# Linear attention and channel mix on one core: queries and attention outputs turned by the transposing DMA

## The chip, the cores and the metric

One core of a Trainium2 chip runs the whole program. The metric is the device time of one execution in microseconds (us); the median of three runs of the kernel before is 203.64 us.

The engines of the core, as the profile names them: PE multiplies matrices (its weight loads are PEld), DVE and ACT work element by element on rows of 128 partitions, POOL and SP here only issue DMAs (and POOL a few constants). PE writes to PSUM, a memory of eight banks, and DVE or ACT must carry its results to SBUF, the working memory. Each engine takes its instructions in order. Engines wait for each other through semaphores.

## The reference

Inputs: q, k, v of shape (8 batches, 8 heads, 576 tokens, 64), a norm vector g of 64, two mixing vectors and three weight matrices.

```python
kv  = einsum('bhsd,bhse->bhde', k, v)
out = einsum('bhsd,bhde->bhse', q, kv)
rms = sqrt(mean(out * out, axis=-1) + 1e-06)
x   = (out / rms * g_norm)            # then heads side by side: (8, 576, 512)

x_prev = x shifted by one token
xk = mu_k * x + (1 - mu_k) * x_prev
xr = mu_r * x + (1 - mu_r) * x_prev
k  = maximum(xk @ w_k, 0)             # 512 -> 1024
v  = (k * k) @ w_v                    # 1024 -> 512
r  = 1 / (1 + exp(-(xr @ w_r)))       # 512 -> 512
result = r * v                        # float32, (8, 576, 512)
```

## The kernel before

The eight batches, numbered 0 to 7 in the code, go one after the other through a pipeline, in bf16. A batch's 576 tokens are laid out as 64 places of 9 tokens: partition p holds tokens 9p to 9p+8, so a load has long rows. Two heads lie above each other in the partitions (64 rows each, "e"), four such pairs side by side. The short names are those of the order string:

- `ld`: load of k, v or q (0, 1, 2) of a batch, issued by POOL (L192), which casts float32 to bf16. Each of in_k, in_v, in_q has one buffer, so a load waits until the batch before it has been read.
- `kv`: k transposed times v on PE (L284), summed over the 9 token groups; `kvo` carries it to SBUF.
- `qt`: q turned on PE, 36 transposes of 64x64 per half (L298); `qto` carries the four quarters to the tile qT (L214 on ACT, L216 on DVE).
- `u`: qT times kv on PE (L320) in three parts; `sq` squares them on ACT (L325), `red` sums the squares on DVE (L329), `nw` are the steps of the inverse root on DVE (L338 to L351), `mul` multiplies u with the root and gives y (L361, DVE).
- `x0`, `x`: y turned on PE (L376), so that channels lie in the partitions; `xo`, `x0o` carry it to the tile xT with the factor g (L366 on ACT, L368 on DVE).
- `wrap` (L532) copies the token before each row's first; `dif` forms the difference of neighbours (L536), `sc` scales it by mu (L542 on ACT, L544 on DVE), `add` adds x (L559), which gives xk and xr.
- `K`: xk times w_k (L572), relu to rt (L564 on ACT, L566 on DVE); `ks` squares rt to sqk (L578, L580). `R`: xr times w_r (L594) and the sigmoid (L597). `V`: sqk times w_v (L604). `fin` multiplies the two (L617, DVE) and stores the result in two DMAs on SP (L620).

A string, ORDER, lists all steps in eight periods. It is written out by hand or by a planner, and nothing reorders it: each engine takes its share of the steps in this order, a step marked ' has its evacuation on DVE and not on ACT, and the digits behind = name the PSUM banks. DMAs are issued where their step stands: loads on POOL, stores on SP. A DMA queue of SP also waits, for every new DMA, until the eighth before it has landed, as eight semaphores go round. xT has two buffers, used by even and odd batches; y, kv and qT have two each, out_sb seven.

Batches 0 and 1 are treated in parts of their own (`qtc`, `uh`, `xh` and the like); the change reaches them only in the shape of a tile.

Of the kernel before, what the change touches and what calls it, by code (L numbers as in the profile page):

```python
# [9 lines left out]
FP32 = mybir.dt.float32  # L10
# [37 lines left out]
    mul.2.2.0 x0.2=70 x0o.2.0 kvo.3.0 V.1.5.0=4 ksp.1.1.4.6 V.1.7.0=2 xo.2.0.4.1' wrap.2 V.1.4.0=7 xo.2.0.4.0'  # L48
    V.1.4.1 x0o.2.1' V.1.5.1 dif.2 sc.2.0.0' sc.2.0.3 sc.2.1.3 qt.3.0=16 qto.3.0.1 sc.2.1.1 qto.3.0.0 fin.1.4
    sc.2.0.1' add.2.0.0 qt.3.1=50 qto.3.1.1 sc.2.0.2' add.2.0.1 sc.2.1.0' qto.3.1.0' kvo.3.1 V.1.6.0=7 V.1.6.1  # L50
    """,
# [5 lines left out]
    nw.3.7.8 ks.2.0' K.2.7.0=1 mul.3.2.0 V.1.8.1 mul.3.1.1 K.2.7.1=4 ks.2.7 x0.3=62 mul.3.0.0 x0o.3.1 ks.2.1'  # L57
    mul.3.1.0 kv.4=51 mul.3.0.1 x.3.0.4=30 xo.3.0.4.1 fin.1.8 x0o.3.0' kvo.4.1' ks.2.2' ld.2.4 qt.4.0=47
    qto.4.0.1' ks.2.5 qto.4.0.0 xo.3.0.4.0' wrap.3 dif.3 sc.3.0.0' qt.4.1=61 V.2.1.0=2 R.2.2=7 sc.3.0.3'
    kvo.4.0' qto.4.1.1' sc.3.0.2 qto.4.1.0 sc.3.1.2' sc.3.0.1' V.2.0.0=0 V.2.2.0=3 ld.0.5 ld.1.5 V.2.0.1  # L60
    add.3.0.0 V.2.1.1 sc.3.1.1 fin.2.0 u.4.1=47 u.4.0=51 sq.4.1.0 add.3.0.1 u.4.2=6 sq.4.2.0 sq.4.0.0 V.2.2.1
    fin.2.1 fin.2.2 sq.4.0.1 red.4.5.9
    """,
# [6 lines left out]
    u.5.1=75 ks.3.0' add.3.1.1 ks.3.5 fin.2.3 ks.3.7 xo.4.0.4.1' wrap.4 u.5.0=10 sq.5.1.1 sq.5.0.0 sq.5.0.1  # L70
    xo.4.0.4.0' dif.4 red.5.5.9 u.5.2=6 sq.5.2.0 R.3.4=2 R.3.5=4 V.3.4.0=3 V.3.4.1 sc.4.0.2 sc.4.1.0 sq.5.1.0
    sc.4.0.1' R.3.6=2 sc.4.0.0' fin.3.4 red.5.0.5 V.3.5.0=4 V.3.5.1 nw.5.0.1 nw.5.1.2 fin.3.5 nw.5.2.3 sc.4.1.2
    nw.5.3.4 nw.5.4.5 nw.5.5.6 add.4.0.0 nw.5.6.7 nw.5.7.8 mul.5.2.0 mul.5.1.0 R.3.7=3 sc.4.0.3 add.4.0.1
    sc.4.1.3 add.4.1.1 V.3.6.0=2 V.3.6.1 R.3.8=4 fin.3.6 mul.5.0.1 V.3.7.0=3 V.3.7.1
# [46 lines left out]
def kernel(  # L121
# [150 lines left out]
    def span(Ms):  # L272
        return slice(2 * Ms[0], 2 * Ms[-1] + 2)

    def kv(a):

        mine(a, "kv", [128, NHP, HD], BF16)
        kb, vb = x_in["k", a], x_in["v", a]
        ps = [take(("kv", a, e), [128, 2, HD], FP32, "ps_kv") for e in range(2)]
        for M in range(2):  # L280
            for j in range(G):
                for e in range(2):
                    for i in range(2):
                        nc.tensor.matmul(ps[e][half(i), M, :], kb[half(e), 2 * M + i, tok(j)],  # L284
                                         vb[half(e), 2 * M + i, tok(j)], start=(j == 0), stop=(j == G - 1))

    def kv_out(a, e, eng):
        evac(eng, at[a]["kv"].rearrange("p (M e) c -> p e M c", e=2)[:, e], give(("kv", a, e)))

    def qt(a, M):  # L290

        mine(a, "qT", [128, NHP, S], BF16)
        qb = x_in["q", a]
        ps = [take(("qt", a, M, e), [128, G, P], BF16, "ps_qt") for e in range(2)]
        for j in range(G):
            for e in range(2):
                for i in range(2):
                    nc.tensor.transpose(ps[e][half(i), j, :], qb[half(e), 2 * M + i, tok(j)], ident[half(e), half(e)])  # L298

    def qt_out(a, M, e, eng):  # L300
        evac(eng, at[a]["qT"][:, 2 * M + e, :], give(("qt", a, M, e)).rearrange("p j c -> p (j c)"))

# [7 lines left out]
    def u(a, part):  # L310

        t0, n = TILES[part]
        ps = [take(("u", a, part, i), [128, max(n, 1), NHP, HD], FP32, "ps_u") for i in range(2 if n else 1)]
        qT_, kv_ = at[a]["qT"], at[a]["kv"]
        for k_ in range(max(n, 1)):
# [252 lines left out]
    def km_part(b, fcs, c0, c1, dst, eng):  # L568
        ps = take("km", [128, len(fcs), c1 - c0], FP32, "ps_km")
        for n, fc in enumerate(fcs):  # L570
            for cc in range(NHP):
                nc.tensor.matmul(ps[:, n, :], wk_sb[:, cc, 128 * fc:128 * fc + 128], at[b]["xk"][:, cc, c0:c1],  # L572
                                 start=(cc == 0), stop=(cc == NHP - 1))
        relu(give("km"), dst, eng)
# [81 lines left out]
    def part_square(b, j, f0, f1, eng):  # L656
# [8 lines left out]
        "qto": lambda eng, a, M, e: qt_out(a, M, e, eng),  # L665
        "u": lambda eng, a, part: u(a, part),
        "sq": lambda eng, a, part, i: square(a, part, i),
# [87 lines left out]
```

## Time and profile before

| What | us |
|---|---|
| Median of three runs (203.59, 203.64, 206.1) | 203.64 |
| Span of the profiled execution, first to last instruction | 201.8 |
| PE busy | 194.5 |
| DVE busy | 164.2 |
| ACT busy | 134.6 |
| L298, transposes of q, busy by the page's reckoning (504 of them) | 6.2 |
| L376, transposes of y (252) | 6.1 |
| L320, u (240) | 5.9 |

Busy times of PE are sums over overlapping instructions of a pipeline: one 64x64 transpose lasts some 190 ns, but 72 of them in a row take about 0.7 us. So the chain of waits, whose pieces stand end to end, is the better measure of what a group of small products costs PE. The row of a group gives the number of instructions, the busy time, the mean of one in ns, and how long the engine stood idle before it and for whom. SP and POOL rows with a q (SPq, POOLq) are issues of DMAs.

### The profile page before, as it was taken

How to read it: one execution, taken by the hardware profiler on the slowest of the kernel's cores; microseconds unless marked ns; L12 is line 12 of the kernel's file. 1: busy time of each engine (PE TensorE's matmuls, PEld its weight loads, DVE VectorE, ACT ScalarE, POOL GpSimd, SP SyncE). 2: the span in 40 equal slices, each digit the busy share in tenths (PEclk: the TensorE clock that was granted, in tenths of full speed). 3: DMA queues.
4: the chain of work that ended last, by engine and by line, in shares of the span. 5: the costliest groups of instructions: out<-in, count | busy, mean ns of one | idle time of the engine just before them, and what ended most of it. 6: DMA issues, size and time to landing. Idle time of an engine off the chain costs nothing.

```text
span 201.8 us, 6347 instructions
## 1 busy us (share of the span) xinstructions
PE 194.5 (96%) x2683; PEld 116.6 (58%) x2683; DVE 164.2 (81%) x360; ACT 134.6 (67%) x281; POOL 27.2 (13%) x44
## 2 busy tenths in 40 slices
PE   7989999999999999999999999999999999999990
PEld 2446754755646766577545765666764565656450
DVE  1499987989998998999999898998969899564341
ACT  3388975869959868798974799675795561416030
POOL 7854103021021004003000040000000000000000
PEclk9999999999999999999999999999999999999999
DMA  6999999999979906991993429901141013420674
GB/s 215 213 206 206 204 206 207 206 184 205 217 119 216 207 27 102 201 256 13 180 238 90 105 27 207 228 1 28 32 107 39 13 40 69 104 52 14 139 164 106
DMA packets 21425, 27.23 MB, mean 135 GB/s; under 512 B 1804, under 2 KB 16404, under 8 KB 21396
## 3 DMA queue, kind: packets, MB, share of 16 engines
q0 software_dynamic: 14912, 16.19, 49.4%
q1 hardware_dynamic: 6164, 10.23, 18.7%
q10 hardware_dynamic: 320, 0.39, 0.9%
q8 instruction: 21, 0.34, 0.7%
q14 instruction: 8, 0.07, 0.1%
HBM read 33.56 MB, written 9.44 MB: 213 GB/s over the span
## 4 chain that ended last, share of the span: by engine, by line
PE 87%; DMA 4%; DVE 2%; POOL 1%; issue 1%; ACT 1%; ACTq 1%; DVEq 0%; POOLq 0%
PE ps_v L604 30%; PE ps_km L572 28%; PE ps_r L594 15%; DMA rt<-in_v_dram 4%; PE ps_qt L298 3%; PE ps_x L376 2%; PE ps_u L320 2%; PE ps_km L644 2%; PE ps_kv L284 2%; PE ps_warm L258 1%; ACTq L620 1%; POOL q L184 1%; ACT sq L486 1%; DVE sqk L580 1%; POOL rt L184 1%
## 5 line engine op out<-in xcount | busy, mean ns | idle before, releaser
L604 PE MATMUL ps_v<-wv_sb,sqk 128*128 128x512 bf16 x280 | 67.1, 379 | 0.3
L572 PE MATMUL ps_km<-xk,wk_sb 128*128 128x288 bf16 (+3 forms) x480 | 64.6, 285 | 0.0
L572 PEld LDWEIGHTS <-wk_sb 128*128 128x128 bf16 x480 | 45.8, 98 | 17.4 <-DVE xk L559 0.3
L564 ACT ACTIVATE rt<-ps_km 128x288 bf16<-128x288 f32 (+3 forms) x93 | 38.5, 431 | 25.2 <-PE ps_km L572 22.1
L604 PEld LDWEIGHTS <-sqk 128*128 128x128 bf16 x280 | 26.4, 98 | 28.9 <-DVE sqk L580 0.4
L594 PE MATMUL ps_r<-wr_sb,xr 128*128 128x512 bf16 x144 | 34.7, 379 | 0.0
L597 ACT ACTIVATE sig<-ps_r 128x512 bf16<-128x512 f32 x36 | 21.1, 609 | 17.5 <-PE ps_r L594 14.8
L617 DVE TENSOR_TENSOR out_sb<-ps_v,sig 128x512 f32<-128x512 f32 (+1 forms) x37 | 24.4, 670 | 7.6 <-ACT sig L597 5.7
L594 PEld LDWEIGHTS <-xr 128*128 128x128 bf16 x144 | 13.8, 98 | 14.6
L578 ACT ACTIVATE sqk<-rt 128x576 bf16<-128x576 bf16 (+2 forms) x27 | 19.5, 730 | 0.2
L542 ACT ACTIVATE m<-dx,cols 128x576 bf16<-128x576 bf16 (+1 forms) x22 | 16.6, 777 | 4.2 <-DVE dx L536 4.2
L329 DVE TENSOR_REDUCE ss<-sq 128x16 f32<-128x1024 bf16 (+1 forms) x12 | 15.9, 1346 | 1.9 <-ACT sq L325 1.8
L361 DVE TENSOR_TENSOR y<-ps_u,rs 128x512 bf16<-128x512 f32 (+1 forms) x30 | 17.2, 629 | 0.2
L580 DVE TENSOR_TENSOR sqk<-rt 128x576 bf16<-128x576 bf16 (+3 forms) x30 | 14.4, 494 | 3.1 <-ACT rt L564 2.9
L566 DVE TENSOR_SCALAR rt<-ps_km 128x288 bf16<-128x288 f32 (+3 forms) x27 | 12.3, 466 | 5.3 <-PE ps_km L572 5.3
L325 ACT ACTIVATE sq<-ps_u 128x512 bf16<-128x512 f32 (+1 forms) x30 | 14.6, 572 | 1.2 <-PE ps_u L320 1.2
L192 POOL DMA_DIRECT2D in_k<-in_k_dram x6 | 4.5, 743 | 79.4 <-PE ps_kv L284 56.1
L544 DVE TENSOR_SCALAR m<-dx,cols 128x576 bf16<-128x576 bf16 (+3 forms) x44 | 14.6, 357 | 0.2
L366 ACT ACTIVATE xT<-ps_x,cols 128x128 bf16<-128x128 bf16 (+3 forms) x17 | 9.1, 563 | 5.0 <-PE ps_x L376 4.9
L536 DVE TENSOR_TENSOR dx<-xT 128x2304 bf16<-128x2304 bf16 (+5 forms) x13 | 11.6, 895 | 0.9 <-ACT xT L366 0.3
L559 DVE TENSOR_TENSOR xr<-m,xT 128x1152 bf16<-128x1152 bf16 x16 | 11.9, 751 | 0.2
L559 DVE TENSOR_TENSOR xk<-m,xT 128x1152 bf16<-128x1152 bf16 (+2 forms) x16 | 10.9, 699 | 0.3
(76 smaller groups left out, 171.5 us busy)
## 6 DMA issues: line engine op xcount, KB each, us to landing
out_dram<-out_sb SPq DMA_DIRECT2D x68, 128.0 KB, 3.4
in_k<-in_k_dram POOLq DMA_DIRECT2D x6, 576.0 KB, 6.6
in_v<-in_v_dram POOLq DMA_DIRECT2D x6, 576.0 KB, 8.9
in_q<-in_q_dram POOLq DMA_DIRECT2D x6, 576.0 KB, 11.0
wk_sb<-in_moe_w_k_dram POOLq DMA_DIRECT2D x2, 512.0 KB, 9.6
sqk<-in_k_dram SPq DMA_DIRECT2D x1, 576.0 KB, 3.8
q<-in_q_dram POOLq DMA_DIRECT2D x2, 288.0 KB, 6.8
sqk<-in_v_dram SPq DMA_DIRECT2D x1, 576.0 KB, 4.7
```

The costliest lines, as they stand in the source:

```text
L329: DVE.tensor_reduce(out=ss[:, g0:g1], in_=sq[:, g0:g1], op=ALU.add, axis=AX.X)
L361: DVE.tensor_mul(out=y[:, g], in0=give(("u", a, part, i)), in1=rs[:, g].unsqueeze(3).to_broadcast([128, max(n, 1), NHP, HD]))
L542: eng.activation(out=out_, in_=in_, func=AF.Copy, scale=mu)
L559: DVE.tensor_add(out=dst, in0=m[:, hs, c0:c1], in1=x[:, hs, c0:c1])
L564: eng.activation(out=dst, in_=ps, func=AF.Relu)
L572: nc.tensor.matmul(ps[:, n, :], wk_sb[:, cc, 128 * fc:128 * fc + 128], at[b]["xk"][:, cc, c0:c1], start=(cc == 0), stop=(cc == NHP - 1))
L578: eng.activation(out=sqk[:, fcs, o:o + n], in_=src, func=AF.Square)
L580: eng.tensor_mul(out=sqk[:, fcs, o:o + n], in0=src, in1=src)
L594: nc.tensor.matmul(ps, xr[:, cc, 128 * t:128 * t + 128], wr_sb[:, cc, :], start=(cc == 0), stop=(cc == NHP - 1))
L597: ACT.activation(out=sig[b, t], in_=give("r"), func=AF.Sigmoid)
L604: nc.tensor.matmul(ps, sqk[:, fc, 128 * t:128 * t + 128], wv_sb[:, fc, :], start=(fc == 0), stop=(fc == NFC - 1))
L617: DVE.tensor_mul(out=o, in0=give(key), in1=sig[b, t][:, c])
```

## The change

Four things are changed together.

1. q of batches 3 to 7 (QD = 3) is no longer turned on PE. A step `qd` issues two transposing DMAs on SP's queue per batch, from in_q (128 partitions x 1152 columns, taken as nine groups of 128 columns) to qT. The steps `qt` and `qto` of these batches go: 360 PE transposes and 20 evacuations.
2. The turned q lies differently: which half of the partitions a token group lies in depends on whether its number is even. So u of these batches (`u_turned`) works in 64x64 quadrants, 72 products instead of 40, and needs kv in both halves of the partitions. kv becomes twice as large, and `kvs` fills its second part: two copies of 64x256 on DVE per batch, which cross to the other half of the partitions.
3. y of batches 4 and 5 (YD) is turned by ten transposing DMAs on SP each (`yd`): two for the first group of tokens, eight for the others. The steps `x`, `x0`, `xo`, `x0o` of these batches go: 72 PE transposes and eight evacuations.
4. A DMA can't multiply by g. So from batch 4 on (WG = 4) xT is left without g, and g goes into copies of w_k and w_r (`wkg_sb`, `wrg_sb`): `wg`, four pieces of 128x1024 and four of 128x512 on DVE, before K.4. The evacuations of xT of batches 6 and 7 become plain copies.

The instructions by engine: PE 2,683 products before and 2,411 after. SP gets 30 transposing DMAs between its stores, in this order: the stores of fin.0.0 to fin.0.3, `qd.3`, five fins (1.4 to 1.8), `qd.4`, fin.2.0 to fin.2.2, `qd.5`, `yd.4`, fin.2.3 and fin.3.4 to fin.3.7, `yd.5`, `qd.6`, fin.3.8 and fin.4.0, `qd.7`, and the others. On POOL the loads of q of batches 4 to 7 wait for the transposing DMAs of the batch before instead of for PE. On DVE, wrap.4 and wrap.5 wait for the last transposing DMA of y. Of ORDER, the steps around are left in place but for these.

The new functions and the places that use them:

```diff
+    QD, YD, WG = 3, (4, 5), 4
+
+    def kv_swap(a, i, eng):
+        kv_ = at[a]["kv"]
+        evac(eng, kv_[half(1 - i), 1], kv_[half(i), 0])
+
+    def q_turn(a, M):
+        qT_ = mine(a, "qT", [128, 2 * G, 128], BF16)
+        nc.sync.dma_start_transpose(out=qT_[:, G * M:G * M + G], in_=x_in["q", a][:, 2 * M:2 * M + 2].rearrange("p m x -> p (m x)"))
+
+    def u_turned(a, part):
...
+                    for h in range(2 if n else 1):
+                        b = G * (2 * (ct // 2) + i) + (2 * (t0 + k_) + 1 + h if n else 0)
+                        r = b % 2
+                        out_ = ps[i][half(h), k_, ct, :] if n else ps[0][half(i), 0, ct, :]
+                        nc.tensor.matmul(out_, qT_[half(r), b // 2, half(ct % 2)], kv_[half(r), 0 if r == i else 1, ct, :],
+                                         start=True, stop=True)
+
+    def y_turn(a):
+        y, x = at[a]["y"], xT[a % 2]
+        for i in range(2):
+            nc.sync.dma_start_transpose(out=x[:, i::2, P:2 * P], in_=y[half(i), 0].rearrange("p n d -> p (n d)"))
+        for t in range(NHP):
+            for i in range(2):
+                c0 = 2 * P + 128 * t
+                nc.sync.dma_start_transpose(out=x[:, i::2, c0:c0 + 128], in_=y[:, 1 + 2 * t + i].rearrange("p n d -> p (n d)"))
+
+    def weights(which, cc, eng):
+        dst, src = ((wkg_sb, wk_sb), (wrg_sb, wr_sb))[which]
...
+            eng.tensor_scalar(out=dst[:, cc], in0=src[:, cc], scalar1=g_sb, scalar2=None, op0=ALU.mult)
...
-    def move(eng, dst, src):
-        if eng is ACT:
+    def move(eng, dst, src, a=0):
+        if a >= WG:
+            evac(eng, dst, src)
+        elif eng is ACT:
             eng.activation(out=dst, in_=src, func=AF.Copy, scale=g_sb)
...
-                nc.tensor.matmul(ps[:, n, :], wk_sb[:, cc, 128 * fc:128 * fc + 128], at[b]["xk"][:, cc, c0:c1],
+                nc.tensor.matmul(ps[:, n, :], (wkg_sb if b >= WG else wk_sb)[:, cc, 128 * fc:128 * fc + 128], at[b]["xk"][:, cc, c0:c1],
...
-            nc.tensor.matmul(ps, xr[:, cc, 128 * t:128 * t + 128], wr_sb[:, cc, :],
+            nc.tensor.matmul(ps, xr[:, cc, 128 * t:128 * t + 128], (wrg_sb if b >= WG else wr_sb)[:, cc, :],
```

And in ORDER, around the two turned batches (the same places before and after):

```diff
-    sc.3.1.3' x0.4=40 qt.5.1=75 x0o.4.0 sc.3.1.0' add.3.1.0 qt.5.0=62 qto.5.0.1' ks.3.6 K.3.7.0=3 ld.0.6
-    K.3.7.1=4 qto.5.1.1 V.2.3.0=2 V.2.3.1 kvo.5.0 ks.3.1' x0o.4.1 ks.3.3' qto.5.1.0' x.4.0.4=34 qto.5.0.0
+    sc.3.1.3' qd.5.0 qd.5.1 sc.3.1.0' add.3.1.0 ks.3.6 K.3.7.0=3 ld.0.6 K.3.7.1=4 V.2.3.0=2 V.2.3.1 kvo.5.0
+    kvs.5.0' kvs.5.1' ks.3.1' ks.3.3' yd.4 u.5.1=75 ks.3.0' add.3.1.1 ks.3.5 fin.2.3 wg.0.2' wg.0.3' ks.3.7
...
-    add.4.1.0 x0.5=16 x.5.0.4=24 x0o.5.1 x0o.5.0 qt.6.1=03 kv.6=75 ld.0.7 qt.6.0=61 xo.5.0.4.1' wrap.5
-    xo.5.0.4.0 dif.5 ks.4.0 qto.6.1.1 K.4.6.1=4 ks.4.6 kvo.6.1' R.4.0=2 R.4.1=3 qto.6.1.0' V.3.8.0=4 sc.5.0.3'
+    add.4.1.0 yd.5 qd.6.0 qd.6.1 kv.6=75 ld.0.7 wrap.5 dif.5 ks.4.0 K.4.6.1=4 ks.4.6 kvo.6.1' R.4.0=2 R.4.1=3
+    V.3.8.0=4 sc.5.0.3' ks.4.5' sc.5.0.0' K.4.7.0=5 sc.5.0.2' sc.5.0.1' kvo.6.0 kvs.6.0' kvs.6.1' add.5.0.1
```

More of the change, by code (lines that the diff above doesn't have):

```diff
@@ L57 @@
     nw.3.7.8 ks.2.0' K.2.7.0=1 mul.3.2.0 V.1.8.1 mul.3.1.1 K.2.7.1=4 ks.2.7 x0.3=62 mul.3.0.0 x0o.3.1 ks.2.1'
[L58 to L62, printed above, removed]
+    mul.3.1.0 kv.4=51 mul.3.0.1 x.3.0.4=30 xo.3.0.4.1 fin.1.8 x0o.3.0' kvo.4.1' ks.2.2' ld.2.4 qd.4.0 qd.4.1
+    ks.2.5 xo.3.0.4.0' wrap.3 dif.3 sc.3.0.0' V.2.1.0=2 R.2.2=7 sc.3.0.3' kvo.4.0' kvs.4.0' kvs.4.1' sc.3.0.2
+    sc.3.1.2' sc.3.0.1' V.2.0.0=0 V.2.2.0=3 ld.0.5 ld.1.5 V.2.0.1 add.3.0.0 V.2.1.1 sc.3.1.1 fin.2.0 wg.0.0'
+    u.4.1=47 u.4.0=51 sq.4.1.0 add.3.0.1 u.4.2=6 sq.4.2.0 sq.4.0.0 V.2.2.1 fin.2.1 fin.2.2 wg.0.1' sq.4.0.1
+    red.4.5.9
     """,
@@ L287, in kv_out, with by_pair @@
     def kv_out(a, e, eng):
[L288 removed]
+        evac(eng, at[a]["kv"][:, 0].rearrange("p (M e) c -> p e M c", e=2)[:, e], give(("kv", a, e)))
+    def kv_swap(a, i, eng):
[5 more added lines that the diff above has]
+    def u_turned(a, part):
+        t0, n = TILES[part]
+        ps = [take(("u", a, part, i), [128, max(n, 1), NHP, HD], FP32, "ps_u") for i in range(2 if n else 1)]
+        qT_, kv_ = at[a]["qT"], at[a]["kv"]
+        for k_ in range(max(n, 1)):
+            for ct in range(NHP):
+                for i in range(2):
[10 more added lines that the diff above has]
+        for t in range(NHP):
+            for i in range(2):
+                c0 = 2 * P + 128 * t
+                nc.sync.dma_start_transpose(out=x[:, i::2, c0:c0 + 128], in_=y[:, 1 + 2 * t + i].rearrange("p n d -> p (n d)"))
+    def weights(which, cc, eng):
+        dst, src = ((wkg_sb, wk_sb), (wrg_sb, wr_sb))[which]
+        if eng is ACT:
+            ACT.activation(out=dst[:, cc], in_=src[:, cc], func=AF.Copy, scale=g_sb)
+        else:
+            eng.tensor_scalar(out=dst[:, cc], in0=src[:, cc], scalar1=g_sb, scalar2=None, op0=ALU.mult)
+    def by_pair(qT_):
+        return qT_.rearrange("p c x -> p (c x)").rearrange("p (n s) -> p n s", n=NHP)
     def qt(a, M):
[L292 removed]
+        mine(a, "qT", [128, 2 * G, 128], BF16)
         qb = x_in["q", a]
@@ L665 @@
         "qto": lambda eng, a, M, e: qt_out(a, M, e, eng),
-        "u": lambda eng, a, part: u(a, part),
+        "u": lambda eng, a, part: (u_turned if a >= QD else u)(a, part),
+        "kvs": lambda eng, a, i: kv_swap(a, i, eng),
+        "qd": lambda eng, a, M: q_turn(a, M),
+        "yd": lambda eng, a: y_turn(a),
+        "wg": lambda eng, which, cc: weights(which, cc, eng),
         "sq": lambda eng, a, part, i: square(a, part, i),
```

61 lines of the change are left out of this document (31 added, 30 removed).

## The prediction

> **What bounds the kernel now.** The list of cores gives a span of 201.8 us at a granted TensorE clock of 0.998, so nothing is throttled. The page's first part and its chain come next:
>
> ```profile
> PE 194.5 (96%) x2683; PEld 116.6 (58%) x2683; DVE 164.2 (81%) x360; ACT 134.6 (67%) x281; POOL 27.2 (13%) x44
> ...
> PE 87%; DMA 4%; DVE 2%; POOL 1%; issue 1%; ACT 1%; ACTq 1%; DVEq 0%; POOLq 0%
> ```
>
> From 33 us to 193 us the chain lists PE pieces alone, end to end: what leaves PE shortens the kernel, if nothing else arrives late. The second thing to read is how near that is. The busy times by stretch:
>
> ```profile
> core 0: us, PE busy (x) PEld busy (x) DVE busy (x) ACT busy (x) POOL busy (x), PEclk, DMA share, GB/s
> ...
> 83.00:112.00 29.00, 29.00 (x413) 17.91 (x412) 27.61 (x57) 22.60 (x50) 2.23 (x3) 1.00 0.79 157
> ```
>
> DVE is busy 27.61 of 29.00 us in the stretch that prepares K.4: it is hardly less of a bound there than PE. The chain in that stretch (start, length, what) prices the removed work and shows its neighbours:
>
> ```profile
> 93.61 0.17 PE ps_x L376 x4
> 93.78 0.71 PE ps_qt L298 x72
> ...
> 97.30 0.57 PE ps_x L376 x32
> 97.87 0.71 PE ps_u L320 x40
> ...
> 109.91 6.37 PE ps_km L572 x52
> 116.28 0.63 PE ps_x L376 x36
> 116.91 0.41 PE ps_qt L298 x36
> ```
>
> **What goes (gain).** Batches are numbered from 0, as in the code. The chain's pieces: q of batch 3 0.73 us, and 0.10 by which the ps_v piece behind it is longer than its usual 1.73 (PE changes its tile shape); q of 4 0.76; q of 5 0.71; q of 6 0.41 + 0.33; q of 7 0.41 + 0.41 and two changes of shape, 0.2. y of 4: 0.17 + 0.57; y of 5: 0.63. Sum 5.4 us of PE: 1.6 by u.4, 3.0 by u.5, 4.4 by u.6. u itself costs the same: its 32 products 64x128 started 14.5 ns apart and its 8 quadrant products 17 ns apart, 0.6 us and one change of shape; now 72 in 64x64, which at the 8.1 ns of L413's 36 take 0.58.
>
> Those 36 read both row halves and write both into one bank (ps_kv of each pair), as the new u does, and four quadrants still ran at once (36 started within 0.28 us). [...]
>
> ACT and DVE lose 20 evacuations of qT and eight of xT (0.4 to 1.1 us each); this hides under PE for ACT. DVE gets ten copies of kv (64x256, like L532's 0.23 us, 0.15 from start to start) and, all before K.4, four of w_k (about 0.40) and four of w_r (0.27), estimated from L544's 0.36 for 576 columns and its slope: 2.7 + 1.5 added, 9 x 0.37 + 3 x 0.66 = 5.3 removed. Over the kernel that is nothing, but between wrap.4 and K.4 it is four w_r copies (1.1) against one evacuation (0.66).
>
> **What comes.** Thirty transposing DMAs on SP, which issues in order: two per q, ten per y. No row of the trace shows one. One q half moves 295 KB in 128 x 9 source pieces of 256 bytes; a y piece of 256 columns has 256 such pieces. Bounds for one:
> - Not below SP's issue, 0.55 us (the median below).
> - By bytes: q1 moved 10.23 MB in 18.7% of 201.8 us, 271 GB/s, so 1.1 us for a q half, 0.24 for a y piece.
> - By packets: the two 256-byte packets in the trace (loads of g_norm) took 31 ns each; 1152 x 31 / 16 engines = 2.2 us, and 0.5 for y. At q1's mean packet, 98 ns, 7.1 and 1.6.
>
> I take 2.2 and 0.55, because the 256-byte packet is the nearest row in size, and 2.0 us from the last issue to landing (the 64 KB stores).
>
> [...]
>
> **Where they lie.** Rows for the places (SP's stores; POOL's issue of in_q for batches 4 and 5; its landing; fin.1.8 and wrap.4 on DVE; the queue and the small stores):
>
> ```profile
> L620 SPq DMA_DIRECT2D out_dram<-out_sb x70: 466/548/1830, 39.3 to 198.1; - x70
> ```
> ```profile
> 61.47 0.74 POOL L192 DMA_DIRECT2D in_q<-in_q_dram  x1 [4.47 <-PE ps_qt L298]
> ...
> 78.57 0.76 POOL L192 DMA_DIRECT2D in_q<-in_q_dram  x1
> ```
> ```profile
> DMA to landing us min/median/max: 9.7/11.0/15.2
> ```
> ```profile
> 75.84 0.68 DVE L617 TENSOR_TENSOR out_sb<-ps_v,sig 128x512 f32<-128x512 f32 x1
> ```
> ```profile
> 98.77 0.23 DVE L532 COPY xT<-xT 128x252 bf16<-128x252 bf16 x1
> ```
> ```profile
> q1 hardware_dynamic: 6164, 10.23, 18.7%
> ...
> out_dram<-out_sb SPq DMA_DIRECT2D x2, 64.0 KB, 2.0
> ```
>
> First chain. in_q has one buffer, so each load of q waits until the batch before it is turned. In the instruction order qd.4 stands on SP behind the two stores of fin.1.8: 76.5 + 1.1 = 77.6. Turned: 77.6 + 4.4 + 2.0 = 84.0, where u.4 is due at 83.4 - 1.6 = 81.8. Only then can POOL load q of 5 (was 78.57): 84.0 + 9.7 = 93.7. qd.5 is issued by 98.1 and lands at 100.1; u.5 was due at 97.9 - 3.0 = 94.9, so PE stands 5 us in all. yd.4 is behind it on SP: 98.1 + 10 x 0.55 = 103.6, landed 105.6. wrap.4 on DVE waits for the last of them, and behind it in DVE's order stand dif.4, the reductions and the root of batch 5, fin.3.4 and fin.3.5, the scalings and sums that K.4 needs. That took 109.9 - 98.8 = 11.1 us of DVE, now 11.5. K.4 starts at 117.1, 7.2 us later than before. On SP the stores of fin.2.3 and the next stand behind qd.5 and yd.4; out_sb has seven buffers, so DVE feels that only when seven are held.
>
> Second chain, from K.4. yd.5 stands behind the stores of fin.3.7 (K.4 + 3.05, then 1.1): 121.3; issued by 126.8, landed 128.8. wrap.5 was at K.4 + 7.85 = 125.0, so DVE waits 3.8 us. qd.6 is behind yd.5: 126.8 + 4.4 + 2.0 = 133.2. u.6 was at K.4 + 12.9, less 1.4 of removed work: 128.6. So u.6 runs at 133.2, 10.4 us later than before. The second chain's DVE wait is covered by this: wrap.5 to kvs.6, which u.6 needs as well, is 3.4 us, 132.2.
>
> After u.6 only q of 7 is left to gain, 1.0 us. Its transposes (load at 133.2, landed 142.9, turned 149.3) are hidden: u.7 comes at about 157. q of 3 is hidden too: loaded at 45.5 + 11.0 = 56.5, turned 62.9, u.3 due at 63.0.
>
> Sum: +10.4 - 1.0 = +9.4 us on the profiled execution, 201.8 of span and 1.8 around it, which is the median, 203.6: **213 us**.
>
> **Rivals.**
> 1. The transposes cost no more than their issue, 0.55 each. For: SP issued the 576 KB loads of k and v in 0.47 us each, little more than small ones. Against: 1152 pieces for a q half. First chain: 77.6 + 1.1 + 2.0 = 80.7; load 90.4; qd.5 lands 93.5, in time; yd.4 97.0 + 2.0 = 99.0; K.4 at 110.5. Second: yd.5 114.6 + 5.5 + 2.0 = 122.1, kvs.6 + 3.4 = 125.5 for u.6, +2.7; less 1.0: 205.3. Without any latency it ends near 202, as DVE then holds K.4. Chance 0.27.
> 2. The other side: everything is hidden and the full 5.4 us is gained, 198.2. It decides if yd.4 lands before about 96 and yd.5 before K.4 + 7, and if DVE gives K.4 its 3 us back. For: SP is idle most of the time. Against: yd.5 needs ten issues after mul.5 and wrap.5 is right behind, and DVE's 27.61 of 29.00. Chance 0.05.
> 3. SP is held in proportion to size. POOL's issue grows with it: 0.57 us for 128x576, 1.03 for 128x2048. With 1.03 per y piece and 4.5 times that per q half: 77.6 + 9.2 + 2.0 = 88.8; 98.5; 107.7; landed 120.0; K.4 131.5; yd.5 146.0; qd.6 157.2, which is +34.4, less 1.0: 237. For: 30 instructions in one order. Against: SP's own rows hardly depend on size. Chance 0.23, from 226 up (98 ns per packet would give 262). [...]
>
> **How the numbers follow.** The forecast's case (1.1 to 3.5 us per q half) has 0.45: at 1.1 the same two chains give 207.5, at 3.5 and 0.8 they give 226. A measurement of this kernel can tell about 2%, 199.6 to 207.7. Slower: 0.45 + 0.23 = 0.68. Within: 0.27. Faster: 0.05. The range leaves out rival 2 and the part of rival 3 above 230: 202 to 230; the forecast's own case is 207 to 226.
>
> **What would show it.** In the changed profile: qT<-in_q on SP at 77 to 79 us and in_q's next load at its landing; wrap.4 near 105; PE idle before ps_u of batches 5 and 6, released by DMA; about 5 us less PE work. It is wrong if a q half lands within 3 us of its issue, if SP issues ten y pieces in much less or more than 5.5 us, or if K.4 waits for something other than the chain from wrap.4.

## The result, and the profile after

The changed kernel took 239.9 us (median of four runs, 237.6 to 241.7) against 204.3 for the kernel before on the same chip: 1.168 times the time, with an interval of 1.156 to 1.180. The prediction had the sign, and missed the size by 27 us.

The profiled execution took 240.7 us with a span of 238.9. One remark on the times below: in some executions the last load of batch 0 lands 1.7 us later and all that follows about 3 us later (the profiles of q alone, of q first, of the products of zeros and of six held are such, the last also of its slowest run, 234.5 us), so I compare these from the u of batch 2 on (46.5 us without it).

First the page: busy times, the granted clock in 40 slices, the queue of SP's DMAs, the engines' shares of the chain.

```profile
PE 196.7 (82%) x2385; PEld 115.8 (48%) x2411; DVE 163.3 (68%) x366; ACT 127.7 (53%) x265; POOL 27.2 (11%) x44
...
PEclk9999999999959998699985799659999999999999
...
q1 hardware_dynamic: 23252, 14.37, 27.5%
...
PE 62%; DMA 14%; SPq 9%; DVE 7%; ACT 3%; issue 3%; POOL 1%; DVEq 0%; POOLq 0%
```

PE carries 62% of the chain where it carried 87%; DMAs, SP's issues and DVE have the rest. PE is busy 2.2 us *longer* than before, though 5.4 us of its work are gone: the clock row says why. It was 9 all through (0.998 in the mean), and now falls behind each of the long waits (0.929). The waits themselves (who waited, for whom, us in total, times, longest):

```profile
POOL in_q L193 <- DMA qT<-in_q: 38.1, 4, 14.4
DVE xT L581 <- DMA xT<-y: 23.0, 2, 12.8
...
PE ps_km L621 <- DVE kv L217: 10.9, 1, 10.9
PE ps_u L314 <- DMA qT<-in_q: 10.7, 4, 6.9
PE ps_r L643 <- DVE out_sb L666: 10.0, 2, 8.8
```

Both predicted chains are there: u waits for the turned q (second to last row), and wrap (L581) waits for the turned y, 10.3 and 12.8 us; the PE waits of 8.8 and 10.9 us are for DVE work that stands behind wrap in DVE's order. What is wrong is their length. SP in order of time (start, length, what):

```profile
56.13 7.60 SPq L300 DMA_TRANSPOSE qT<-in_q  x2
...
84.63 8.53 SPq L300 DMA_TRANSPOSE qT<-in_q  x2
...
104.28 2.74 SPq L300 DMA_TRANSPOSE qT<-in_q  x2
107.13 3.14 SPq L321 DMA_TRANSPOSE xT<-y  x2
110.37 10.88 SPq L325 DMA_TRANSPOSE xT<-y  x8
...
140.95 2.53 SPq L321 DMA_TRANSPOSE xT<-y  x2
143.58 11.74 SPq L325 DMA_TRANSPOSE xT<-y  x8
```

Ten pieces of y hold SP for 14.1 and 14.4 us, not 5.5 (hold: the time for which issuing DMAs occupies SP; landing: the time from the start of an issue until the data has arrived). The same by tile (issue min/median/max in ns, first and last start; then landing after issue, in us), y and then q:

```profile
L325 SPq DMA_TRANSPOSE xT<-y x16: 1189/1244/2662, 110.4 to 154.1; - x16
L321 SPq DMA_TRANSPOSE xT<-y x4: 1179/1219/1907, 107.1 to 142.3; - x4
...
DMA to landing us min/median/max: 2.3/4.6/10.0
```
```profile
L300 SPq DMA_TRANSPOSE qT<-in_q x10: 1253/1404/5887, 56.1 to 168.8; - x10
...
DMA to landing us min/median/max: 3.3/5.7/9.8
```

A q half has 4.5 times the columns of a y piece, and its smallest issue is nearly the same, 1.25 against 1.18 us. And landings run from 2.3 to 10 us. So two questions: is the hold of SP one per instruction whatever its size, and what makes a landing take 10 us? How late each mark came:

| Mark | before | predicted | after | late |
|---|---|---|---|---|
| u of batch 4 on PE | 83.3 | 84.0 | 95.5 | 12.2 |
| u of batch 5 | 97.7 | 100.1 | 111.5 | 13.8 |
| wrap.4 on DVE | 98.8 | 105.6 | 124.5 | 25.7 |
| u of batch 6 | 122.8 | 133.2 | 161.2 | 38.4 |
| end of the span | 201.8 | 211.2 | 238.9 | 37.1 |

By stretches: from u of batch 2 to u of batch 5 the changed kernel takes 13.8 us more than before, from there to u of batch 6, where both turned y lie, 24.7 more (49.7 against 25.1), and from there to the end 1.4 less.

### The profile page after: what moved, and what is told of

Same layout as the page of the kernel before. It is cut to its first block, busy times and chain, and to the rows that moved or that the text cites. A ratio compares the mean times of both kernels' runs of the same rounds, so it can differ in the third digit from the quotient of the medians.

```text
span 238.9 us, 5816 instructions
## 1 busy us (share of the span) xinstructions
PE 196.7 (82%) x2385; PEld 115.8 (48%) x2411; DVE 163.3 (68%) x366; ACT 127.7 (53%) x265; POOL 27.2 (11%) x44
## 4 chain that ended last, share of the span: by engine, by line
PE 62%; DMA 14%; SPq 9%; DVE 7%; ACT 3%; issue 3%; POOL 1%; DVEq 0%; POOLq 0%
PE ps_km L621 23%; PE ps_v L653 19%; PE ps_r L643 10%; SPq L325 7%; DMA qT<-in_q 7%; DMA rt<-in_v_dram 3%; DMA out_dram<-out_sb 2%; PE ps_km L693 2%; PE ps_u L314 2%; DVE dx L585 2%; PE ps_x L425 2%; PE ps_kv L287 2%; DVE sqk L629 1%; DMA xT<-y 1%; DVE out_sb L666 1%
## 5 line engine op out<-in xcount | busy, mean ns | idle before, releaser
L653 PE MATMUL ps_v<-wv_sb,sqk 128*128 128x512 bf16 x262 | 68.7, 397 | 2.0 <-issue 1.0
L621 PE MATMUL ps_km<-xk,wkg_sb 128*128 128x288 bf16 x256 | 35.4, 288 | 11.0 <-DVE kv L217 10.9
L653 PEld LDWEIGHTS <-sqk 128*128 128x128 bf16 x280 | 27.5, 101 | 31.6 <-issue 4.5
L666 DVE TENSOR_TENSOR out_sb<-ps_v,sig 128x512 f32<-128x512 f32 (+1 forms) x37 | 24.6, 670 | 18.9 <-PE ps_v L653 13.3
L621 PEld LDWEIGHTS <-wkg_sb 128*128 128x128 bf16 x256 | 24.9, 98 | 21.3 <-issue 11.2
L621 PE MATMUL ps_km<-xk,wk_sb 128*128 128x288 bf16 (+3 forms) x224 | 31.8, 296 | 0.5 <-ACT kv L215 0.4
L621 PEld LDWEIGHTS <-wk_sb 128*128 128x128 bf16 x224 | 22.2, 103 | 9.9 <-issue 1.9
L643 PE MATMUL ps_r<-wr_sb,xr 128*128 128x512 bf16 x69 | 18.4, 399 | 10.1 <-DVE out_sb L666 10.0
L643 PEld LDWEIGHTS <-xr 128*128 128x128 bf16 x144 | 14.1, 100 | 25.5 <-issue 11.8
L372 ACT ACTIVATE sq<-ps_u 128x512 bf16<-128x512 f32 (+1 forms) x30 | 14.6, 562 | 14.4 <-PE ps_u L314 14.4
L581 DVE COPY xT<-xT 128x252 bf16<-128x252 bf16 x8 | 2.0, 252 | 23.5 <-DMA xT<-y 23.0
L643 PE MATMUL ps_r<-wrg_sb,xr 128*128 128x512 bf16 x69 | 16.9, 379 | 0.3 <-issue 0.2
L629 DVE TENSOR_TENSOR sqk<-rt 128x576 bf16<-128x576 bf16 (+3 forms) x30 | 14.4, 496 | 3.1 <-ACT rt L613 2.9
L615 DVE TENSOR_SCALAR rt<-ps_km 128x288 bf16<-128x288 f32 (+3 forms) x27 | 12.2, 464 | 6.1 <-PE ps_km L621 6.1
L314 PE MATMUL ps_u<-kv,qT 64*64 64x64 bf16 x360 | 5.9, 216 | 10.7 <-DMA qT<-in_q 10.7
```

Of the source, the lines that this page charges most:

```text
L621: nc.tensor.matmul(ps[:, n, :], (wkg_sb if b >= WG else wk_sb)[:, cc, 128 * fc:128 * fc + 128], at[b]["xk"][:, cc, c0:c1], start=(cc == 0) ...
L629: eng.tensor_mul(out=sqk[:, fcs, o:o + n], in0=src, in1=src)
L643: nc.tensor.matmul(ps, xr[:, cc, 128 * t:128 * t + 128], (wrg_sb if b >= WG else wr_sb)[:, cc, :], start=(cc == 0), stop=(cc == NHP - 1))
L653: nc.tensor.matmul(ps, sqk[:, fc, 128 * t:128 * t + 128], wv_sb[:, fc, :], start=(fc == 0), stop=(fc == NFC - 1))
L666: DVE.tensor_mul(out=o, in0=give(key), in1=sig[b, t][:, c])
```

## The experiments

Each median stands beside its ratio to the kernel before on the same chip. The names: a "q half" is one of the two DMAs of a batch's q, a "y piece" one of the ten of a batch's y.

### The parts alone

q alone, with y back on PE and g back in the evacuations:

```diff
-    QD, YD, WG = 3, (4, 5), 4
+    QD, YD, WG = 3, (), 8
```

> Only q of batches 3 to 7 goes through the transposing DMA; y of batches 4 and 5 is turned on PE again and g stays in the evacuations (no copies of the weights). Theory A (two separate chains, one by q, one by y): in the changed kernel u.4 stood at 95.5 us against 83.4 before, +12, and u.5 at 111.5 against 97.9, +13.6, so the q chain alone is worth +13 by u.5; q of 6 and 7 are then loaded in time and their 1.5 us of PE work is gained: 203.6 + 12 = 216 us (212 to 219). Rival (the q transposes on SP are the whole loss, y is late only because it is queued behind them): +30, 232 or more.

217.7 us, 1.067 (1.058 to 1.076).

y alone, with the g copies:

```diff
-    QD, YD, WG = 3, (4, 5), 4
+    QD, YD, WG = 8, (4, 5), 4
```

> Only y of batches 4 and 5 goes through the transposing DMA, with the g copies that this needs; every q is turned on PE again. Theory A (SP is held about 1.25 us by every transposing DMA whatever its size, ten of them per y): wrap.4 comes 12.5 + 2.4 us behind the last product of y of 4, about 10 us later than before; wrap.5 about 11 us later; less 1.4 us of PE work, plus some us of lower clock after the waits: 222 to 230 us, and the ten pieces take 12 us or more of SP each time. Rival (y pieces are late only behind the q transposes): 205 to 210, ten pieces in about 5.5 us.

231.7 us, 1.134 (1.126 to 1.143). SP in order of time:

```profile
91.83 2.54 SPq L321 DMA_TRANSPOSE xT<-y  x2
94.47 12.55 SPq L325 DMA_TRANSPOSE xT<-y  x8
...
126.87 2.52 SPq L321 DMA_TRANSPOSE xT<-y  x2
129.50 11.54 SPq L325 DMA_TRANSPOSE xT<-y  x8
```

With no q transpose ahead of them, the ten pieces still take 14 to 15 us: y is a chain of its own.

The g copies alone:

```diff
-    QD, YD, WG = 3, (4, 5), 4
+    QD, YD, WG = 8, (), 4
```

> Nothing is turned by DMA; only the copies of w_k and w_r with g (eight scalings on DVE before K.4) and the plain evacuations from batch 4 on are kept. Theory: about 2.9 us of DVE work added where DVE has about 1.4 us of slack before K.4, less nothing: 204 to 206. Rival (DVE is the bound before K.4 and the copies alone are a good part of the loss): 207 or more.

205.4 us, 1.006 (1.002 to 1.009). The eight scalings took 0.48 and 0.34 us each, 3.3 in all, and cost half of that.

q alone and the copies came out in the ranges of the theory of two separate chains, y alone 1.7 us above its range. Added up, +13.9 and +27.9 (with its copies), they give 41.8 where the whole change lost 36 to 37. That the waits overlap a little would explain it; no run tried this.

### What a transposing DMA costs by itself

The kernel before, with unused transposes between its stores:

```diff
+        elif kind >= 6:
+            nc.sync.dma_start(out=dst.rearrange("p n x -> p (n x)"), in_=src[:, c0:c0 + 128 * n])
+        else:
+            nc.sync.dma_start_transpose(out=dst, in_=src[:, c0:c0 + 128 * n])
```

> The kernel before with transposing DMAs that nothing uses, from the SBUF copy of q of batch 0 to a scratch tile, on SP between its stores: two of 128x1152 behind fin.1.4 and four of 128x256 behind fin.1.7, while k, v and q of the next batch are being loaded; and late in the kernel, when no load runs, four of 128x256, two of 128x1152, one of 128x2304, two of 128x128, two of 64x256, two of 128x512, and three plain SBUF to SBUF copies (two of 128x256, one of 128x1152). Theory A (a fixed hold): SP is held 1.2 to 1.3 us by every transposing DMA from 64x256 to 128x1152 when no load runs, 0.5 us by a plain copy. Rival B (by size): 128x1152 holds it 4.5 times as long as 128x256, 128x128 half as long. On the loads: theory C (the loads' packets slow the transposes down), 2.5 to 5 us for 128x1152 among loads and 1.3 without; rival D (the long ones come from the q tile itself), 1.3 in both places.

203.9 us in one run: SP has room for all of them. SP in order of time; L291 are the transposes of 128 partitions (scr_a: 128x1152 twice at 61 and at 151 us, 128x2304 at 156; scr_b: 128x256 four times at 70 and at 140, 128x128 at 165, 128x512 at 175), L287 the 64x256 and L289 the plain copies:

```profile
61.53 5.14 SPq L291 DMA_TRANSPOSE scr_a<-q  x2
...
70.72 5.88 SPq L291 DMA_TRANSPOSE scr_b<-q  x4
...
151.22 2.80 SPq L291 DMA_TRANSPOSE scr_a<-q  x2
...
156.00 2.76 SPq L291 DMA_TRANSPOSE scr_a<-q  x1
...
165.72 2.52 SPq L291 DMA_TRANSPOSE scr_b<-q  x2
...
170.46 2.46 SPq L287 DMA_TRANSPOSE scr_b<-q  x2
...
175.58 2.55 SPq L291 DMA_TRANSPOSE scr_b<-q  x2
...
179.50 1.18 SPq L289 DMA_DIRECT2D scr_b<-q  x2
180.72 0.60 SPq L289 DMA_DIRECT2D scr_a<-q  x1
```

From 64x256 to 128x1152 a transpose holds SP for 1.2 to 1.4 us when no load runs (one of the 128x256 at 140 us took 2.3), a plain copy of the same bytes 0.6. Only at 128x2304 does the hold grow, to 2.8. So far theory A. But theory C holds in kind too: among the loads, the two of 128x1152 held SP for 1.7 (less than the 2.5 expected) and 3.4 us and landed 8.2 and 9.0 us after their issue, at 69.8 and 72.3; the load of q in flight then landed at 71.4. Pieces of 128x256 late in the kernel landed in 2.3.

### Fewer pieces, and loads out of the way

If the hold of SP is one per piece, fewer pieces of the same y must help. Six instead of ten:

```diff
-        for t in range(NHP):
-            for i in range(2):
-                c0 = 2 * P + 128 * t
-                nc.sync.dma_start_transpose(out=x[:, i::2, c0:c0 + 128], in_=y[:, 1 + 2 * t + i].rearrange("p n d -> p (n d)"))
+        yy = y.rearrange("p g n d -> p (g n d)")[:, 256:]
+        for hp in range(NHP):
+            nc.sync.dma_start_transpose(out=x[:, hp, 2 * P:].rearrange("p (t c) -> p t c", c=128),
+                                        in_=yy[:, 512 * hp:512 * hp + 512])
```

> The changed kernel with the same y turned in six transposing DMAs per batch instead of ten: the two of the first token group as they were, and four of 128x512 (one per pair of heads) in place of eight of 128x256; the product that makes y writes it in that order. Same bytes, fewer instructions. Theory A (each transposing DMA holds SP 1.25 us whatever its size, and that hold is what makes wrap.4 and wrap.5 late): five us less at each of the two, 239.9 - 10 = 229 to 231 us. Theory C (the pieces land only when the loads of k, v, q that are in flight have landed, in the changed kernel at 119 to 123 us and 154 us, whatever SP does): 236 to 239. Rival B (SP is held by size): no change, 239 to 241.

240.3 us, 1.178 (1.173 to 1.183): nothing gained. This alone would have spoken for the hold by size. The landings decide otherwise (y, as above):

```profile
L324 SPq DMA_TRANSPOSE xT<-y x8: 1212/1656/3767, 111.3 to 149.5; - x8
L321 SPq DMA_TRANSPOSE xT<-y x4: 1203/1252/1952, 108.0 to 143.1; - x4
...
DMA to landing us min/median/max: 6.4/8.9/11.6
```

The smallest hold of a piece twice as large is still 1.2 us, but every one of the eight takes 6.4 us or more to land. Set beside the loads of k, v and q that POOL had issued shortly before or meanwhile (times of landing, us):

| Kernel | last load in flight landed | transposes behind it landed |
|---|---|---|
| changed, q of 3 | v of 4: 65.5 | 66.0, 66.9 |
| changed, y of 4 | q of 6: 123.0 | 123.0, 123.3; wrap.4 at 124.5 |
| changed, y of 5 | v of 7: 154.4 | 155.4 to 156.4 |
| six pieces, y of 4 | q of 6: 125.0 | 125.5, 126.0 |
| six pieces, y of 5 | v of 7: 154.8 | 155.1 to 155.9 |

The last transposes of a group land just behind the loads in flight; the first can land before the last load (118.7 and 120.5 for y of 4 in the changed kernel). Then each of two limits hides the other: for y of 4 the ten holds end at 121 us and the loads at 123, for y of 5 the holds at 155.3 and the loads at 154.4. The next two runs hold the loads of batches 6 and 7 back until y of 4 and of 5 has landed, with ten pieces and with six:

```diff
+    def gate(a):
+        POOL.tensor_copy(out=gate_sb, in_=xT[a % 2][:, :, P + 63::64])
...
-    sc.3.1.3' qd.5.0 qd.5.1 sc.3.1.0' add.3.1.0 ks.3.6 K.3.7.0=3 ld.0.6 K.3.7.1=4 V.2.3.0=2 V.2.3.1 kvo.5.0
-    kvs.5.0' kvs.5.1' ks.3.1' ks.3.3' yd.4 u.5.1=75
+    sc.3.1.3' qd.5.0 qd.5.1 sc.3.1.0' add.3.1.0 ks.3.6 K.3.7.0=3 K.3.7.1=4 V.2.3.0=2 V.2.3.1 kvo.5.0
+    kvs.5.0' kvs.5.1' ks.3.1' ks.3.3' yd.4 gt.4 ld.0.6 u.5.1=75
...
-    add.4.1.0 yd.5 qd.6.0 qd.6.1 kv.6=75 ld.0.7
+    add.4.1.0 yd.5 qd.6.0 qd.6.1 kv.6=75 gt.5 ld.0.7
```

> The changed kernel, y in ten pieces as there, but the loads of k, v and q of batch 6 are issued only when y of batch 4 has landed, and those of batch 7 only when y of batch 5 has (POOL copies a few columns of xT to a scratch tile first, which makes it wait). Theory (two limits side by side: SP is held 1.25 us per piece, and a transpose lands only behind the loads in flight): with the loads gone the ten holds of SP still end near 120 us and 153 us, so wrap.4 and wrap.5 come only 1 to 3 us earlier: 236 to 239 us, with the pieces landing 2.4 us after their issue. Rival C alone (only the loads hold the pieces): 10 us less, 229 to 231.

> The same with y in six pieces. Theory (two limits side by side): six holds of 1.25 us and 2.4 us to land, so y of 4 lands about 117 us instead of 124.3 and y of 5 about 5.5 us earlier than in the changed kernel: 240 - 12 = 227 to 230 us, though six pieces alone changed nothing (240.3). Rival (a piece takes 8 us to land whatever else moves): 238 to 241.

Ten held: 238.0 us, 1.165 (1.161 to 1.169). Six held: 227.0 us, 1.111 (1.107 to 1.116). The pieces of the first, then of the second:

```profile
L325 SPq DMA_TRANSPOSE xT<-y x16: 1189/1243/2249, 109.2 to 151.8; - x16
...
DMA to landing us min/median/max: 2.3/2.4/4.2
```
```profile
L324 SPq DMA_TRANSPOSE xT<-y x8: 1213/1265/2250, 117.1 to 147.7; - x8
...
DMA to landing us min/median/max: 2.4/2.4/4.0
```

Six pieces alone: nothing. Loads held back alone: 2 us, which the two intervals can't tell from nothing. Both: 13 us. Without the loads a piece lands in 2.4 us in the median, and then the number of holds shows in the time: ten pieces hold SP for 14.8 and 13.9 us, six for 8.7 and 9.2, 10.8 less in all, and the two kernels differ by 11.0.

The stretch from u of batch 5 to u of batch 6 says the same in the profiles:

| Kernel | us |
|---|---|
| before | 25.1 |
| changed | 49.7 |
| six pieces | 46.8 |
| ten, loads held | 45.9 |
| six, loads held | 37.9 |

Here each edit alone gives 3 to 4 us and both together 12. In the profile of the six pieces the 3 us are lost again ahead of it, where u of batch 3 came 2.3 us later with its q. So the length of the y chain has two causes side by side, the holds of SP and the loads in flight, and each hides most of what the other costs.

### The clock behind the waits

In windows of the changed kernel (from:to and length, then PE, PEld, DVE, ACT, POOL busy, the granted clock, DMA share, GB/s) PE runs at half its clock for some 7 us behind the wait of 2.7 us before u of batch 3:

```profile
60.00:66.00 6.00, 3.28 (x18) 1.51 (x16) 5.23 (x12) 2.31 (x6) 0.00 (x0) 1.00 1.23 204
66.00:72.00 6.00, 5.04 (x85) 3.29 (x87) 2.03 (x3) 2.58 (x6) 0.74 (x1) 0.50 1.05 232
72.00:78.00 6.00, 6.00 (x44) 4.32 (x43) 4.14 (x12) 3.81 (x10) 0.00 (x0) 0.93 0.23 62
```

The granted clock is 0.50 in the 6 us behind the wait and 0.93 in the 6 us after that. What does this cost in the end? Products of zeros in three waits keep PE going:

```diff
-    K.2.0.0=6 sc.2.1.2' K.2.0.1=1 u.3.0=50
+    K.2.0.0=6 sc.2.1.2' K.2.0.1=1 wm.10=5 u.3.0=50
...
-    u.4.1=47
+    wm.30=4 u.4.1=47
...
-    K.4.7.0=5
+    wm.48=1 K.4.7.0=5
```

> The changed kernel with products of zeros on PE in three of its waits, so that PE does not stand still there: 10 before u.3, 30 before u.4, 48 before the first K product behind the wait of 10.9 us in K.4; each 128x512, 0.215 us at full clock, all together shorter than the waits. Theory (PE's clock falls after a wait: the pieces behind these three waits were 4 to 5 us longer than the same pieces before): 235 to 236 us, and a granted clock near 1.0 behind these waits. Rival (the longer pieces wait for something else): 239 to 241, or more by the added products.

239.0 us, 1.172 (1.166 to 1.178), against 1.168 (1.156 to 1.180) without: by the medians no gain that can be told, though the clock was there behind the three waits (1.00 from 66 to 97 and from 160 to 172 us; behind the wait between them, left as it was, it fell again, to 0.89 in the mean of 125 to 160). The same window of time, changed kernel first:

```profile
66.00:97.00 31.00, 22.47 (x337) 13.99 (x344) 18.55 (x41) 14.28 (x29) 2.39 (x4) 0.83 0.75 137
```
```profile
66.00:97.00 31.00, 28.32 (x383) 16.24 (x387) 20.86 (x45) 14.58 (x31) 2.23 (x4) 1.00 0.91 156
```

The profiles say more than the medians. From u of batch 3 to u of batch 5, behind the first two of these waits, the kernel with the products takes 41.5 us, the changed kernel 45.5 and the other four profiles with the same transposes of q there 44.5 to 45.4: the clock was worth 3 to 4 us in this stretch. From u of batch 5 to u of batch 6, with the third, it takes 50.2 against 49.7: there the chain runs over SP, DMAs and DVE, and PE, when faster, waits the longer for them. From u of batch 2 to the end 189.2 us stand against 192.4. So the lower clock probably costs some 3 us of the 36; four runs of each kernel, which scatter by 3 to 4 us, can't confirm it.

### q with its loads in order

The q part alone, with each load of q ahead of the loads of k and v of its batch, and the transposes earlier on SP (batch 4 shown):

```diff
-    ks.2.3' ld.0.4 ld.1.4 K.2.5.1'=7 K.2.6.0=2 K.2.6.1=1 V.1.8.0=7
+    ks.2.3' ld.2.4 ld.0.4 ld.1.4 qd.4.0 qd.4.1 K.2.5.1'=7 K.2.6.0=2 K.2.6.1=1 V.1.8.0=7
...
-    mul.3.1.0 kv.4=51 mul.3.0.1 x.3.0.4=30 xo.3.0.4.1 fin.1.8 x0o.3.0' kvo.4.1' ks.2.2' ld.2.4 qd.4.0 qd.4.1
+    mul.3.1.0 kv.4=51 mul.3.0.1 x.3.0.4=30 xo.3.0.4.1 fin.1.8 x0o.3.0' kvo.4.1' ks.2.2'
```

> As the kernel with q alone on the transposing DMA (217.7), but every load of q from batch 4 on is issued ahead of the loads of k and v of its batch, so that k and v wait until the q before has been turned, and the transposes of q of 4 to 7 are issued earlier on SP (4 behind fin.1.7, 5 ahead of fin.2.0, 6 behind fin.2.3, 7 behind fin.3.8). Theory C (a transpose lands late because loads are in flight, and the chain through the single q buffer carries that on): q of 3 lands by about 61 us, q of 4 by 78, q of 5 by 93, all before they are needed at 63, 82 and 95; PE no longer waits at u, and about 3.6 us of its work are gone: 200 us (199 to 202). Rival (a q half needs 8 us from issue to landing in any case): u.3 is 3 us late, the rest in time: 203 to 205. Rival (the u product in 64x64 quadrants costs what the transposes saved): 203 to 204.

208.5 us, 1.015 (1.009 to 1.020): more than any of the three expectations, though nine less than q alone, and PE no longer waits for a turned q. With no load in flight the halves of batch 3 landed in 3.4 and 3.3 us, at 62.8 and 64.1; those of batch 4 at 80.9 and 81.9, right behind v of 4 (80.0), and u of 4 came at 86.8. But nothing is gained: from u of batch 2 to the end the profile has 155.6 us against 155.3 before, for 3.5 us less of PE's busy time. The u of 64x64 quadrants explains little of this: it starts its 72 products over 0.7 us for batches 4 and 5, as the 40 before, and over 0.85 and 0.87 us for 6 and 7; only u of 3 takes 1.5, with a wait for DVE in it.

Only the q of batches whose transposes have time:

```diff
-    QD, YD, WG = 3, (4, 5), 4
+    QD, YD, WG = 6, (), 8
```

> Only q of batches 6 and 7 through the transposing DMA, at the places of the change; all else as before. Both transposes are issued when few loads run and u.6 and u.7 come 10 us later or more, so they are hidden in every theory but the one in which the u product in 64x64 quadrants eats the gain: 202 us (201.5 to 202.5), against 203.5 to 204 by that rival.

202.5 us, 0.994 (0.992 to 0.996): 1.3 us faster than before. The halves of q (issue in ns, landing in us) as the prediction wanted all of them:

```profile
L300 SPq DMA_TRANSPOSE qT<-in_q x4: 1291/1378/1395, 115.2 to 132.9; - x4
```

They landed 3.3 to 3.5 us after issue, and nobody waited.

Batch 5 as well, its load first and its transposes ahead of fin.2.0:

```diff
-    V.2.2.0=3 ld.0.5 ld.1.5 V.2.0.1 add.3.0.0 V.2.1.1 sc.3.1.1 fin.2.0
+    V.2.2.0=3 ld.2.5 ld.0.5 ld.1.5 V.2.0.1 add.3.0.0 V.2.1.1 sc.3.1.1 qd.5.0 qd.5.1 fin.2.0
```

> q of batches 5, 6 and 7 through the transposing DMA, the load of q of 5 ahead of k and v of 5, its transposes ahead of fin.2.0 on SP; 6 and 7 at the places of the change. Theory: q of 5 lands by 92 us, u.5 is due at 97.7, so 0.7 us of PE work more are gained than with 6 and 7 alone (202.5): 201.5 to 202.2. Rival (DVE, 27.6 of 29.0 us busy before K.4, gives nothing back for PE work taken away there): 202.5 or a little more.

203.4 us, 0.997 (0.995 to 0.998): 0.7 less PE work, 0.9 us more time. DVE in order of time shows a wait that neither the prediction nor I had so far (start, length, what, idle before and for whom):

```profile
94.02 0.76 DVE L608 TENSOR_TENSOR xr<-m,xT 128x1152 bf16<-128x1152 bf16 x1
96.35 0.69 DVE L217 COPY kv<-kv 64x256 bf16<-64x256 bf16 x2 [1.57 <-ACT kv L215]
```

The copies of kv (kvs) stand right behind an evacuation of kv on ACT, and DVE, which prepares K.4, stands still for it. Moved behind work that is ready:

```diff
-    kvo.5.0 kvs.5.0' kvs.5.1' ks.3.1' x0o.4.1 ks.3.3'
+    kvo.5.0 ks.3.1' x0o.4.1 ks.3.3' kvs.5.0' kvs.5.1'
...
-    kvo.6.0 kvs.6.0' kvs.6.1' add.5.0.1
+    kvo.6.0 add.5.0.1 kvs.6.0' kvs.6.1'
```

> As the kernel with q of 5, 6 and 7 (203.4), but the copies of kv stand later in DVE's order: those of batch 5 behind two squares of K.3, those of batch 6 behind a sum of batch 5. Theory (the copies' wait for ACT, 1.6 us at batch 5 and 0.7 at batch 6, held DVE's work for K.4): no DVE wait for kv, wrap.4 back near 99 us, 201.3 to 202.3 us. Rival (DVE holds K.4 whatever the order): 203 to 203.7.

202.4 us, 0.992 (0.989 to 0.995). One microsecond of the 1.6 came back (wrap.4 at 99.3 instead of 100.2); 0.8 us of the wait are left.

> As the kernel with q of 6 and 7 (202.5), with the copies of kv of batch 6 behind a sum of batch 5. Theory: up to 0.7 us of a DVE wait goes, behind which PE mostly does not stand: 202.0 to 202.5. Rival: no difference, 202.5.

202.7 us, 0.994 (0.991 to 0.997): no difference for batch 6 alone.

> As the kernel with all q of 3 to 7, loads of q first (208.5, its body from u.2 on 0.3 us longer than before, its start 3 us later in most executions), with the copies of kv of batches 3, 5 and 6 later in DVE's order. Theory: some 2 us of DVE waits go before K.3 and K.4: 205.5 to 207, that is 2 us less. Rival: 208 to 209.

205.0 us, 1.001 (0.996 to 1.006). Less than the 208.5, but of the difference the body from u of batch 2 to the end has only 0.4 us (155.2 against 155.6 in the profiles); the rest lies ahead of u of batch 2, where the two kernels are the same, so this run doesn't settle it. One new wait is named in it, PE for the load of v of batch 4, which now goes behind q:

```profile
PE ps_kv L287 <- DMA in_v<-in_v_dram: 1.6, 1, 1.6
```

Where the other 2 us of the removed 3.5 to 4 us of PE time go when all of q is turned by DMA stays open.

### The whole change, repaired

Loads of q first, transposes earlier, six pieces, loads of the next batch behind y; the edits are those above.

> The whole change (q of 3 to 7, y of 4 and 5, the g copies) with what the runs so far ask for: loads of q ahead of k and v, the q transposes earlier on SP, y in six pieces, loads of the next batch behind y. Theory: the q part costs nothing any more (as in the kernel with q alone so ordered), and what is left is y: six holds and the landing after the last product of y, 7.5 + 2.4 us, against 2 us on PE, about 7 us at each of wrap.4 and wrap.5, and the g copies 1.6: 216 to 222 us. Rival (the parts disturb each other in a way not seen yet): above 225.

218.4 us, 1.070 (1.067 to 1.075). Pieces of y:

```profile
L324 SPq DMA_TRANSPOSE xT<-y x8: 1260/1264/2054, 99.8 to 130.5; - x8
L321 SPq DMA_TRANSPOSE xT<-y x4: 1169/1206/1253, 97.3 to 124.5; - x4
...
DMA to landing us min/median/max: 2.4/2.4/3.2
```

21 of the 36 us are gone. What stays is y: the last product of y, six holds and 2.4 us put wrap.4 at 106.7 against 98.8 before, and nothing hides that. From u of batch 5 to u of batch 6 it still takes 39.0 us, 13.9 more than before.

## Why the prediction was wrong, step by step

- **What bounds the kernel, and the two chains.** Right. qd.4 behind fin.1.8, in_q's single buffer, qd.5, yd.4, wrap.4, K.4, and then yd.5, wrap.5, u.6 are the places of the waits in the profile after; q alone and y alone lose by themselves.
- **The hold of SP per piece: the step that failed most.** The text priced a y piece at 0.55 us by its 256-byte packets, and SP's rows for plain DMAs stood for its issue. A transposing DMA holds SP for 1.2 us even at 64x256 and 128x128 (the probe), and one or two of the ten for about 2 or more, so ten took 14 us instead of 5.5, one of the signs of being wrong that the text had named. The packets were not the limit of a piece: the 16,128 packets of 256 bytes that the changed kernel adds to the trace took 18 ns in the median, not 31, which gives an estimate of 0.3 us for 256 of them over 16 engines. A q half without loads was *cheaper* than priced, 1.25 to 1.4 us instead of 2.2. In the terms of the first chain: wrap.4 came at 124.5 instead of 105.6, and of these 18.9 us 9.0 are the later start of yd.4 (107.1 instead of 98.1, by the q chain), 8.6 the ten holds, and 1.3 the time behind the last of them (3.3 instead of 2.0). yd.5 added another 8.9 us of holds.
- **"2.0 us from the last issue to landing": the other step that failed.** Near enough without loads, 2.3 to 2.4 from the start of the issue for a piece and 3.3 for a q half; among loads 8 to 10 us. The row came from the last stores of the kernel, when nothing is loaded. At the places of q of 3 and 4 and of both y, 576 KB loads were in flight, and the page before showed DMA busy there (6 to 9 tenths). "q of 3 is hidden" (turned by 62.9) fell to this: 66.9. qd.4 then started at 84.6 instead of 77.6, and among the loads of batch 5 its two holds took 8.5 us instead of 4.4.
- **The rivals.** Rival 3 gave 237, near the result, by a wrong mechanism: SP is not held in proportion to size up to 128x1152. The POOL row that it rested on was misread as well: 1.03 us for 128x2048 is the mean of 1.31 and 0.76, and another load of that size took 0.76. That the time agreed would have passed for proof; the probe and the six pieces showed that it is none. Rivals 1 and 2 needed landings near 2 us.
- **Work removed from PE, 5.4 us, and u at no cost.** The rate of u was right: the 64 quadrant products of u of 7 started 8 ns apart, as the 36 of L413 in the kernel before did (8.1), not 17. But where the eight of the first group come first, as in u of 6 and 7, mostly a gap of 0.22 to 0.25 us stands behind them, and these two are 0.1 to 0.2 us longer; u of 4 and 5 in the kernel with the loads of q first, without such a gap, are as long as before.
- **DVE's added work, "over the kernel nothing".** The copies with g are 3.3 us, not 2.7, and cost 1.6. The copies of kv were counted by their own 0.23 us; their wait for ACT, 1.6 us at batch 5, was not looked for.
- **Not foreseen:** the half clock behind waits. By the profiles it cost some 3 us ahead of u of batch 5; behind it, where PE was not what ended last, none showed.

## What to carry to other kernels

Price a kind of DMA that the trace does not show by two separate numbers, the hold of its queue and the landing, and take the landing from rows in the same traffic as the place where it will stand, not from a quiet end of the kernel. When cutting a suspected cost changes nothing, look for a second limit that ends just behind it before giving up the first, and read the stretch where it lies besides the total: here six pieces gained 0, held loads 2, both 13 us. Here the transposing DMA paid where the result was wanted well after it had landed (q of the last two or three batches: 202.4 to 202.5 us, the best versions found; with two, q landed 3.3 to 3.5 us after its issue, and u of 6 came 7.6 us after the first one), not between a product and its only reader (y: 231.7 us alone).

## What the hardware showed

- A transposing DMA between SBUF places holds SP 1.2 to 1.4 us from 64x256 to 128x1152, and 2.8 us at 128x2304; plain copies hold it 0.6. Single ones of 1.9 to 2.7 us stand between (up to 3.8 at 128x512, among loads), without loads too (2.3 in the probe, 2.2 with ten held), and what makes them is open. At 18 ns for a packet of 256 bytes (the median in the changed kernel), 16 engines would need 1.3 us for 128x1152 and 2.6 for 128x2304, an estimate: the two largest may be held by their packets.
- It lands 2.3 us (128x256) to 3.5 us (128x1152) after its issue when nothing is loaded. Behind 576 KB loads in flight the last of a group lands mostly 0.3 to 2 us after them, up to 11.9 us after its issue (q of 3 in the kernel with six pieces), and 128x1152 then holds SP for up to 6.4 us. Why was not tried.
- PE's granted clock is 0.50 for 3 to 7 us behind the four waits of 2.7 to 10.9 us in the changed kernel, and 1.00 again after that.
